# Half as many products of zeros in each unit of the first group, and another table of ranks, in a planned attention and expert kernel

## The chip, the cores and the metric

The kernel runs on one core of a Trainium2 chip. The metric is the device time of one execution in microseconds (us). Before the change it is 705.01 us, the median of three runs (704.97 to 705.55).

## The reference

Three layers follow each other. Causal attention over 2 batches, 8 heads, 576 tokens and 64 dimensions is mixed by a gate per head with a memory read; two dense layers with an ELU follow, and then four experts that are all computed and weighted by token.

```python
scores = np.where(causal, -1e9, (q @ k.T) / np.sqrt(D)); a = softmax(scores)
local = a @ v                                            # attention
mem_out = (phi(q) @ M_prev) / (phi(q) @ z_prev + 1e-6)   # phi(x) = elu(x) + 1
x = g * mem_out + (1 - g) * local                        # to 1152 x 512
h = x @ w_in;  x = elu(h) @ w_out                        # 512 -> 2048 -> 512
out = sum_e p[:, e] * (np.maximum(x @ w1[e], 0) @ w2[e]) # 4 experts, 512 -> 1024 -> 512
```

## The kernel before, in words

Every dense product is made of three (`mm3`, L319 to L321): numbers are split into a high and a low part, and high by high, low by high and high by low are summed in PSUM. The tiles are `ua` and `da` for the first dense pair, `ub` and `db` for the experts, with 384 or 512 columns. A weight block of 128x1024 is loaded, copied to its high part on ScalarE (`wh`, L283) and subtracted on GpSimd for the low part (`wl`, L287). The blocks of the first dense pair come as 64-bit numbers that are converted first: ScalarE's L263 and VectorE's L269 and L273. From block 5 on this conversion holds one of the two PSUM banks of the scores meanwhile (`cv`, tags `s0` and `s1`).

Attention is cut into units. Four units F0 to F3 (the first group) hold the first 192 tokens of both batches, one for each pair of heads; eight units R00 to R13 hold the rest, one for each batch and pair. A unit's steps are: load; split (`qh` on ScalarE, `ql` on GpSimd, on VectorE for F0); feature map `pp`; memory product into bank `om` (`mem`, L1331) with its division on VectorE; then for each of three query tiles a score (L1382), a masked minimum on VectorE (`lowest`, L1396) and an exponential on ScalarE (L1405); transposes in groups of four (`trans`, L1444) into the one PSUM bank `t`; its evacuation on ScalarE or VectorE in turn (`evac`, L1451 and L1449); value products into bank `ov` (L1460, L1467); the division, the sum with the memory part (L1499) and a last transposition (`turn`, L1505). F units also use banks of the three `m` for half of their scores and transposes; R units have `s0`, `s1` and `t` alone.

A planner (class `Plan`) fixes the order on each engine before anything runs. Every step has an engine, a cost, a rank and the steps that it follows; `MOVES` adds to ranks by family of step. Walking a modelled clock, it gives each engine the startable step of lowest rank. TensorE prefers to stay where it is, in attention or in dense work: it turns to the other kind only if the first startable step of its own kind ranks later by more than `STAY[0]` (in attention) or `STAY[1]` (in dense work). The engines then run these queues in order, and wait on semaphores.

TensorE also multiplies zeros: a product of zeros (`nothing`, L345) is 128x512 in bfloat16, writes a bank that the next step then overwrites, and stands there to keep TensorE busy. Eleven stand at the start (`warm`). `keep_busy(ps, least)` issues the larger of `least` and a number that the planner sets where its modelled TensorE waits over 0.3 us in the first 140 us. `FEWEST` is the `least` of a unit: one for F, none for R. A unit of F has it in six places: two of its three scores, the memory product, both groups of transposes, and the first value product.

Of the kernel before, what the change touches and what calls it, by code (L numbers as in the profile page):

```python
# [53 lines left out]


MOVES = {
# [15 lines left out]
}  # L72


# [19 lines left out]
def tile_kernel(  # L94
# [112 lines left out]
    FEWEST = {"F": 1, "R": 0}  # L207
# [136 lines left out]
    def nothing(ps):  # L344
        nc.tensor.matmul(  # L345
            ps.rearrange("p (n k) -> p n k", k=P), zeros, zeros.unsqueeze(1).to_broadcast([P, ps.shape[1] // P, P]),
            start=True, stop=True,
        )
# [3 lines left out]
    def keep_busy(ps, least=0):  # L352

        for _ in range(max(waits[0], least)):
            nothing(ps)
        waits[0] = 0

    def atile(shape, dtype, tag, name):
        return at["sbuf"].tile(shape, dtype, tag=tag, name=name, bufs=SLOTS[tag])

    def abank(tag, name):

        if tag == "m":
            return ps_m.tile([P, 512], F32, tag="m", name=name)
        return at[tag[0]].tile([P, 512], F32, tag=tag, name=name)
# [6 lines left out]
    class Moe1:  # L372

        parts, kind = NPART, "a"
# [169 lines left out]
    class Moe2(Moe1):  # L544

        parts, kind = 2 * E, "b"
# [234 lines left out]
    keep = {}  # L781
# [97 lines left out]
    class Wide1(Wide):  # L879
        parts, kind = NPART, "a"  # L880
# [117 lines left out]
    class Wide2(Wide):  # L998
        parts, kind = 2 * E, "b"
# [79 lines left out]
    def act_cost(n, psum=False):  # L1079
        return 0.833e-3 * n + (0.055 if psum else 0.095)  # L1080

    def dve_cost(n):
        return 1.042e-3 * n + 0.065
# [4 lines left out]
    def values_cost(kind, blocks):  # L1088

        return 0.06 * (kind == "F") + 0.203 * sum(2 if kind == "F" and (t, odd) == (2, 2) else 1 for t, odd, _ in blocks)  # L1090

    STAY = [18.6, 8.4]
    TURN = 0.09

    def attends(key):
# [2 lines left out]
    class Plan:  # L1098
# [4 lines left out]
        def __init__(self, slots):  # L1103
# [3 lines left out]

            self.stay = {True: STAY[0], False: STAY[1]}

# [100 lines left out]
    def segments(ext):  # L1210
        return [(0, ext)] if ext <= 512 else [(0, 288), (288, 576)]

    def plan_unit(plan, kind, b, c, start, spare, slack):
# [6 lines left out]
        unit, uid = {}, f"F{c}" if kind == "F" else f"R{b}{c}"  # L1220

        def parts_of(t):

            if kind == "F":
                return [(t, 0, P)] if t < 2 else [(0, 0, D), (1, D, D)]
            return [(0, 0, P)]

        def add(key, engine, cost, fn, after=(), takes=(), gives=()):
            step = key.rstrip("0123456789")
            plan.add(  # L1230
                (uid, key), engine, cost, start + OFFSET[step], fn,
                [(uid, a) if isinstance(a, str) else a for a in after], takes, gives,
                slack.get(engine, 0.0) + LANDING * (step in ("split_h", "phi_r") and uid not in ("F0", "F1")),
                early=EARLY if kind == "R" else 1e9,
            )
# [50 lines left out]
        for name, cs, loaded in splits:  # L1286
            n, first = cs.stop - cs.start, name == splits[0][0]
# [68 lines left out]
        def row(odd, t):  # L1356

            ext = tiles[t][1]
            first = 2 * base[t] + odd * ext
            return unit["pt"][:, first:first + ext]  # L1360

        def score(t, n):
            ext = tiles[t][1]
            a, z_ = segments(ext)[n]
            w = z_ - a
            if "pt" not in unit:
                unit["pt"] = atile([P, 2 * widest], F32, tag="pt", name=f"pt{uid}")[:, :2 * width]
                unit["nm"] = [atile([P, 6], F32, tag="nm", name=f"nm{uid}{odd}") for odd in (0, 1)]
            for odd in (0, 1):
                tag = "m" if "m" in s_from[t, n] else f"s{odd}"  # L1370
                unit["s", odd, t, n] = abank(tag, f"s{uid}{odd}{t}{n}")
            keep_busy(unit["s", 0, t, n], FEWEST[kind] * (t != 1))
            for bi, r0, r in parts_of(t):

                q = slice(qcol[t] + r0, qcol[t] + r0 + P)
                k0 = nq + bi * nkeys
                ks = slice(k0 + a, k0 + z_), slice(k0 + nkeys - ext + a, k0 + nkeys - ext + z_)
                final = r0 + r == P
                for m, (x, y) in enumerate(("hh", "hl", "lh")):
                    for odd in (0, 1):  # L1380
                        rows = slice(D * odd, D * odd + D)
                        nc.tensor.matmul(  # L1382
                            unit["s", odd, t, n][:, :w], unit[x][rows, q], unit[y][rows, ks[odd]],
                            start=m == 0 and r0 == 0, stop=m == 2 and final,
                        )
# [19 lines left out]
            nc.scalar.activation(out=blk, in_=blk, func=AF.Exp, scale=-1.0, bias=unit["nm"][odd][:, k:k + 1])  # L1405

        def score_cost(t, w):
            return len(parts_of(t)) * max(3 * w / 2400, 0.32) + 0.24 + 0.22 * FEWEST[kind] * (t != 1)

        for t, n, a, z_ in pieces:  # L1410
            first, last = (t, n) == pieces[0][:2], (t, n) == pieces[-1][:2]
# [23 lines left out]

        def transposes(g):
            pst = unit["t", g] = abank(t_from[g], f"t{uid}{g}")
            keep_busy(pst, FEWEST[kind])
            for n, (t, odd, j) in enumerate(groups[g]):
                if odd == 2:  # L1440
                    src = unit["pt"][:, 2 * base[t] + P * j:2 * base[t] + P * j + P]
                else:
                    src = row(odd, t)[:, P * j + D * odd:P * j + D * odd + P]
                nc.tensor.transpose(pst[:, P * n:P * n + P], src, ident)  # L1444

        def evac(g, col):
            pf = unit["p", g] = atile([P, 512], F32, tag="ph", name=f"pf{uid}{g}")
            if g % 2:
                nc.vector.tensor_copy(pf[:, :col], unit["t", g][:, :col])  # L1449
            else:  # L1450
                nc.scalar.activation(out=pf[:, :col], in_=unit["t", g][:, :col], func=AF.Copy)  # L1451
# [19 lines left out]
        for g, blks in enumerate(groups):  # L1471
            col, final = P * len(blks), g == len(groups) - 1
            add(
                f"trans{g}", "pe", 0.109 * len(blks) + 0.05 * (kind == "F") + 0.22 * FEWEST[kind], lambda g=g: transposes(g),
                sorted({f"exp{t}{odd}" for t, o, _ in blks for odd in ((0, 1) if o == 2 else (o,))})
                + [f"trans{g - 1}"] * (g > 0), [t_from[g]],
                ["pt"] * final,
            )
            add(
                f"evac{g}", "dve" if g % 2 else "act", dve_cost(col) if g % 2 else act_cost(col, True),  # L1480
                lambda g=g, col=col: evac(g, col), [f"trans{g}"], ["ph"],
                [("m", (uid, f"trans{g}")) if t_from[g] == "m" else "t"],
            )
            add(
                f"values{g}", "pe", values_cost(kind, blks) + 0.22 * FEWEST[kind] * (g == 0), lambda g=g: values(g),
                [f"evac{g}", "load_v"] + [f"values{g - 1}"] * (g > 0), ["ov"] * (g == 0), ["ph"] + ["rv", "nm", "nm"] * final,
            )
# [188 lines left out]
```

## Time and profile before

| | before |
|---|---|
| median of three runs | 705.01 us |
| the profiled execution | 705.03 us |
| its span, first to last instruction | 703.2 us |
| granted TensorE clock in every stretch | 1.00 (2.4 GHz) |
| TensorE busy | 697.8 us, 99% |
| VectorE, ScalarE, GpSimd busy | 387.7, 353.8, 426.6 us |

How to read it: the page's span leaves out 1.8 us of the execution. TensorE's busy time counts pipelined products from their start to a modelled end, so neighbours overlap; what a product costs the engine is the distance from its start to the next start, which the timeline shows. Matmuls in float32 (transposes, memory and value products) appear under their own lines.

### The profile page before, as it was taken

What the parts mean: (1) busy time and instruction counts of PE and PEld (TensorE: products, weight loads), DVE (VectorE), ACT (ScalarE), POOL (GpSimd) and SP (SyncE); (2) the same over time, 40 slices, a digit from 0 to 9 for tenths busy, and PEclk for the clock granted to TensorE, in tenths of its full rate; (3) what the DMA queues carried; (4) which work ended last, traced back from release to release, by engine and by line L of the source; (5) the groups of instructions that cost most, each with busy time, mean ns of one, the idle gap of its engine ahead of it and who ended that gap; (6) DMA issues with size and microseconds to landing.
All of it is one profiled execution on the core that took longest, in us unless ns stands there. A gap on an engine that the chain in (4) does not pass through costs nothing.

```text
span 703.2 us, 10662 instructions
## 1 busy us (share of the span) xinstructions
PE 697.8 (99%) x4064; PEld 638.8 (91%) x4064; DVE 387.7 (55%) x847; ACT 353.8 (50%) x611; POOL 426.6 (61%) x256
## 2 busy tenths in 40 slices
PE   9999999999999999999999999999999999999997
PEld 5788999999898998999999999999898989989896
DVE  5887878553434234723736648674554736455462
ACT  7889777654543335444865647633342424233220
POOL 6778766575554552599986564787655666464110
PEclk9999999999999999999999999999999999999999
DMA  8897877533413241234322212031121302111002
GB/s 279 293 307 248 291 243 255 185 121 127 139 60 122 90 131 49 91 119 136 121 64 87 90 45 75 32 116 65 60 91 31 119 29 93 61 60 61 1 0 90
DMA packets 23683, 82.21 MB, mean 117 GB/s; under 512 B 2896, under 2 KB 3152, under 8 KB 23632
## 3 DMA queue, kind: packets, MB, share of 16 engines
q1 hardware_dynamic: 23632, 81.53, 34.9%
q8 instruction: 32, 0.52, 0.3%
q14 instruction: 19, 0.16, 0.1%
HBM read 70.77 MB, written 10.75 MB: 116 GB/s over the span
## 4 chain that ended last, share of the span: by engine, by line
PE 96%; DVE 2%; ACT 1%; issue 0%; POOL 0%; POOLq 0%; DVEq 0%; ACTq 0%
PE db L319 9%; PE db L321 9%; PE db L320 9%; PE da L319 5%; PE da L321 5%; PE da L320 5%; PE ov L1460 4%; PE ub L319 3%; PE ub L321 3%; PE ub L320 3%; PE sR L1382 3%; PE tR L1444 3%; PE ua L319 2%; PE ua L321 1%; PE ua L320 1%; PE ov L1467 1%
## 5 line engine op out<-in xcount | busy, mean ns | idle before, releaser
L287 POOL TENSOR_TENSOR wl<-wr,wh 128x1024 fp32r<-128x1024 f32 x72 | 172.4, 2399 | 157.4 <-ACT wh L283 156.7
L283 ACT ACTIVATE wh<-wr 128x1024 fp32r<-128x1024 f32 x72 | 75.9, 1056 | 101.9 <-PE db L320 61.8
L319 PE MATMUL db<-wh,hb 128*128 128x512 f32 x288 | 112.7, 391 | 0.0
L321 PE MATMUL db<-wl,hb 128*128 128x512 f32 x288 | 112.4, 390 | 0.0
L320 PE MATMUL db<-wh,hb 128*128 128x512 f32 x288 | 112.3, 390 | 0.0
L1049 DVE SCALAR_TENSOR_TENSOR acc<-db,pr,acc 128x512 f32<-128x512 f32 x42 | 31.5, 750 | 70.8 <-PE db L321 70.8
L319 PE MATMUL da<-ha,wh 128*128 128x384 f32 x192 | 65.8, 343 | 0.0
L321 PEld LDWEIGHTS db<-wl,hb 128*128 128x128 f32 x288 | 54.1, 188 | 11.4
L321 PE MATMUL da<-ha,wh 128*128 128x384 f32 x192 | 64.3, 335 | 0.0
L320 PE MATMUL da<-ha,wl 128*128 128x384 f32 x192 | 64.2, 335 | 0.0
L319 PEld LDWEIGHTS db<-wh,hb 128*128 128x128 f32 x288 | 54.1, 188 | 10.8 <-issue 0.2
L320 PEld LDWEIGHTS db<-wh,hb 128*128 128x128 f32 x288 | 54.1, 188 | 10.7
L319 PE MATMUL ub<-yh,wh 128*128 128x384 f32 x128 | 44.6, 349 | 0.0
L321 PE MATMUL ub<-yl,wh 128*128 128x384 f32 x128 | 43.0, 336 | 0.0
L320 PE MATMUL ub<-yh,wl 128*128 128x384 f32 x128 | 42.8, 335 | 0.0
L1460 PE MATMUL ov<-rvR,pfR 128*128 128x65 f32 x288 | 38.6, 266 | 0.0
L1460 PEld LDWEIGHTS ov<-rvR,pfR 128*128 128x128 f32 x288 | 36.9, 191 | 0.9 <-issue 0.8
L557 ACT ACTIVATE hb<-ub 128x384 fp32r<-128x384 f32 x32 | 15.7, 490 | 43.8 <-PE ub L321 43.7
L319 PEld LDWEIGHTS da<-ha,wh 128*128 128x128 f32 x192 | 36.1, 188 | 0.7 <-issue 0.7
L320 PEld LDWEIGHTS da<-ha,wl 128*128 128x128 f32 x192 | 36.1, 188 | 0.0
L321 PEld LDWEIGHTS da<-ha,wh 128*128 128x128 f32 x192 | 36.0, 188 | 0.0
L560 DVE SCALAR_TENSOR_TENSOR hb<-ub,hb 128x384 fp32r<-128x384 f32 x32 | 17.8, 557 | 33.0 <-ACT hb L557 32.7
(859 smaller groups left out, 1833.5 us busy)
## 6 DMA issues: line engine op xcount, KB each, us to landing
wr<-in_w SPq DMA_DIRECT2D x64, 512.0 KB, 3.7
w<-in_w SPq DMA_DIRECT2D x32, 512.0 KB, 5.8
wscr<-wr SPq DMA_DIRECT2D x16, 512.0 KB, 6.5
wr<-wscr SPq DMA_DIRECT2D x16, 512.0 KB, 3.3
rvR<-in_vm_r SPq DMA_DIRECT2D x8, 520.0 KB, 4.6
qkR<-in_qk_r SPq DMA_DIRECT2D x8, 480.0 KB, 4.9
rvF<-in_vm_f SPq DMA_DIRECT2D x4, 520.0 KB, 6.1
out<-acc SPq DMA_DIRECT2D x8, 256.0 KB, 2.0
```

What stands on the lines that cost most here:

```text
L283: nc.scalar.activation(out=t["wh"], in_=t["wr"], func=AF.Copy)
L287: nc.gpsimd.tensor_tensor(out=wl, in0=t["wr"], in1=f32(t["wh"]), op=ALU.subtract)
L319: nc.tensor.matmul(out, ah, bh, start=first, stop=False)
L320: nc.tensor.matmul(out, al, bh, start=False, stop=False)
L321: nc.tensor.matmul(out, ah, bl, start=False, stop=last)
L557: nc.scalar.activation(out=t["h"][:, 0], in_=t["ps"], func=AF.Relu)
L560: nc.vector.scalar_tensor_tensor(out=t["h"][:, 1], in0=t["ps"], scalar=0.0, in1=f32(t["h"][:, 0]), op0=ALU.max, op1=ALU.subtract)
L1049: nc.vector.scalar_tensor_tensor(out=acc, in0=t["ps"], scalar=p, in1=acc, op0=ALU.mult, op1=ALU.add)
L1382: nc.tensor.matmul(unit["s", odd, t, n][:, :w], unit[x][rows, q], unit[y][rows, ks[odd]], start=m == 0 and r0 == 0, stop=m == 2 and final,)
L1444: nc.tensor.transpose(pst[:, P * n:P * n + P], src, ident)
L1460: nc.tensor.matmul(unit["ov"][:, odd, t], pf[:, col:col + P], unit["rv"][:, at_], start=False, stop=odd == 1 and j == nb - 1)
L1467: nc.tensor.matmul(pair("ov", t, r0, r), pf[:, col + r0:col + r0 + r], apart(at_), start=True, stop=nb == 0,)
```

## The change

`FEWEST` counts in three places of a unit instead of six: the memory product, the first group of transposes, and the first value product. The scores and the second group keep only what the planner asks for, and the planner's costs follow. `MOVES` has other entries and values throughout, and `STAY` is 86.268 and 0.703 instead of 18.6 and 8.4. Lines after the table are four higher in the changed kernel.

```diff
 MOVES = {
-    ("F", "evac"): -13.8, ("F", "join_l"): -16.9, ("F", "load"): -51.9, ("F", "mem_a"): 3.9, ("F", "phi_r"): 13,
...
+    ("F", "exp"): 1.027, ("F", "load"): -47.23, ("F", "lowest"): -22.121, ("F", "phi_r"): 12.499,
...
-    STAY = [18.6, 8.4]
+    STAY = [86.268, 0.703]
...
-            keep_busy(unit["s", 0, t, n], FEWEST[kind] * (t != 1))
+            keep_busy(unit["s", 0, t, n])
...
-            return len(parts_of(t)) * max(3 * w / 2400, 0.32) + 0.24 + 0.22 * FEWEST[kind] * (t != 1)
+            return len(parts_of(t)) * max(3 * w / 2400, 0.32) + 0.24
...
-            keep_busy(pst, FEWEST[kind])
+            keep_busy(pst, FEWEST[kind] * (g == 0))
```

The cost of `trans` in the planner gets the same factor `(g == 0)`.

Three places show what the new ranks do. The first is TensorE at unit R02's transposes, groups 1 to 3 (`tR021` to `tR023`), with its value products and the first score of R12. Before:

```order
L1444 MATMUL tR021_2090<-ident_66,ptR02_1898 128x128 x4
L1467 MATMUL ov_121<-rvR02_1591,pfR020_2078 128x130
L1460 MATMUL ov_121<-rvR02_1591,pfR020_2078 128x65 x3
L1382 MATMUL sR12000_2111<-qhR12_2041 128x288
L1382 MATMUL sR12100_2112<-qhR12_2041 128x288
L1382 MATMUL sR12000_2111<-qlR12_2074,qhR12_2041 128x288
L1382 MATMUL sR12100_2112<-qlR12_2074,qhR12_2041 128x288
L1382 MATMUL sR12000_2111<-qhR12_2041,qlR12_2074 128x288
L1382 MATMUL sR12100_2112<-qhR12_2041,qlR12_2074 128x288
L1444 MATMUL tR022_2122<-ident_66,ptR02_1898 128x128 x4
L1460 MATMUL ov_121<-rvR02_1591,pfR021_2103 128x65 x4
L319 MATMUL da0330_2135<-ha030_1654,wh15_1800 128x384
```

Eight more dense products follow this last row before `tR023`. After:

```order
L1448 MATMUL tR021_2031<-ident_66,ptR02_1857 128x128 x4
L1471 MATMUL ov_121<-rvR02_1572,pfR020_2020 128x130
L1464 MATMUL ov_121<-rvR02_1572,pfR020_2020 128x65 x3
L1448 MATMUL tR022_2050<-ident_66,ptR02_1857 128x128 x4
L1464 MATMUL ov_121<-rvR02_1572,pfR021_2043 128x65 x4
L1386 MATMUL sR12000_2069<-qhR12_2029 128x288
L1386 MATMUL sR12100_2070<-qhR12_2029 128x288
L1386 MATMUL sR12000_2069<-qlR12_2047,qhR12_2029 128x288
L1386 MATMUL sR12100_2070<-qlR12_2047,qhR12_2029 128x288
L1386 MATMUL sR12000_2069<-qhR12_2029,qlR12_2047 128x288
L1386 MATMUL sR12100_2070<-qhR12_2029,qlR12_2047 128x288
L1448 MATMUL tR023_2078<-ident_66,ptR02_1857 128x128 x4
```

The nine dense products between groups 2 and 3 are gone from there, and the score moved from ahead of group 2 to ahead of group 3. ScalarE at the same place, from the evacuation of group 0 (`pfR020`) to that of group 2 (`pfR022`). Before:

```order
L1451 ACTIVATE pfR020_2078<-tR020_2064 128x512
L283 ACTIVATE wh19_2087<-wr19_1910 128x1024
L503 ACTIVATE yh0_2100<-da0300_1987 128x384
L503 ACTIVATE yh0_2100<-da0310_2024 128x384
L503 ACTIVATE yh0_2100<-da0320_2049 128x384
L1451 ACTIVATE pfR022_2132<-tR022_2122 128x512
```

After, with the exponentials of R02 and the ELU of `ua` (L448 to L459) ahead and between:

```order
L287 ACTIVATE wh17_1995<-wr17_1909 128x1024
L459 ACTIVATE ha031_1937<-eva0u310_1979 128x384
L1409 ACTIVATE ptR02_1857<-ptR02_1857,nmR020_1858 128x320
L1409 ACTIVATE ptR02_1857<-ptR02_1857,nmR021_1859 128x320
L448 ACTIVATE eva0u320_2017<-ua0320_1984 128x384
L451 ACTIVATE eva0u320_2017<-eva0u320_2017 128x384
L1455 ACTIVATE pfR020_2020<-tR020_1973 128x512
L1254 ACTIVATE qhR12_2029<-qkR12_1485 128x960
L459 ACTIVATE ha032_1983<-eva0u320_2017 128x384
L448 ACTIVATE eva0u330_2045<-ua0330_2006 128x384
L451 ACTIVATE eva0u330_2045<-eva0u330_2045 128x384
L287 ACTIVATE wh18_2055<-wr18_1948 128x1024
```

`ha033` (L459) and `pfR022` (L1455) follow. The split of R12's keys, a weight block and ELU work now stand between the two evacuations. The second place is VectorE after F3's third score (`sF3020`, `sF3120`), whose minimum frees the banks `s0` and `s1` for R00. Before:

```order
L1396 ISA ptF3_498,nmF30_499<-sF3020_540,mask2_79 128x64
L1396 ISA nmF30_499 128x1
L1396 ISA ptF3_498,nmF31_500<-sF3120_541,mask2_79 128x64
L1396 ISA nmF31_500 128x1
L1306 SCALAR_TENSOR_TENSOR nv_F2_578<-ov_121,wloc_96 128x6
L1521 RECIPROCAL nv_F2_578<-nv_F2_578 128x6
L1312 TENSOR_TENSOR tvF2_582<-ov_121,nv_F2_578 128x2x3x64
L273 SCALAR_TENSOR_TENSOR wr1_385<-w64_1_0_293,wr1_385 128x512
L1396 ISA ptR00_584,nmR000_585<-sR00000_587,mask_71 128x288
```

After:

```order
L273 TENSOR_SCALAR wr1_437<-wr1_437 128x512
L277 SCALAR_TENSOR_TENSOR wr1_437<-w64_1_1_403,wr1_437 128x512
L1310 SCALAR_TENSOR_TENSOR nv_F2_568<-ov_121,wloc_96 128x6
L1525 RECIPROCAL nv_F2_568<-nv_F2_568 128x6
L1316 TENSOR_TENSOR tvF2_584<-ov_121,nv_F2_568 128x2x3x64
L1400 ISA ptF3_480,nmF30_481<-sF3020_536,mask2_79 128x64
L1400 ISA nmF30_481 128x1
L1400 ISA ptF3_480,nmF31_482<-sF3120_537,mask2_79 128x64
L1400 ISA nmF31_482 128x1
```

Two conversions of weight block 1 and F2's division moved ahead of the minimum. The third place is TensorE between F3's last value products and R00's memory product, which overwrites bank `om` once F3's last sum (L1499) has read it. Before:

```order
L1467 MATMUL ov_121<-rvF3_470,pfF31_614 64x130 x2
L319 MATMUL ua0000_653<-xh0_100,wh0_458 128x384
L320 MATMUL ua0000_653<-xh0_100,wl0_538 128x384
L321 MATMUL ua0000_653<-xl0_101,wh0_458 128x384
L319 MATMUL ua0000_653<-xh0_100,wh0_458 128x384
L320 MATMUL ua0000_653<-xh0_100,wl0_538 128x384
L321 MATMUL ua0000_653<-xl0_101,wh0_458 128x384
L1382 MATMUL sR00010_671<-qhR00_474 128x448
```

Five more score products and twelve more dense ones stand before the memory product there. After:

```order
L349 MATMUL sR00010_660<-zeros_93 128x512
L1386 MATMUL sR00010_660<-qhR00_477 128x448
L1386 MATMUL sR00110_661<-qhR00_477 128x448
L1386 MATMUL sR00010_660<-qlR00_521,qhR00_477 128x448
L1386 MATMUL sR00110_661<-qlR00_521,qhR00_477 128x448
L1386 MATMUL sR00010_660<-qhR00_477,qlR00_521 128x448
L1386 MATMUL sR00110_661<-qhR00_477,qlR00_521 128x448
L349 LDWEIGHTS zeros_93
L349 MATMUL om_120<-zeros_93 128x512
```

Another product of zeros stands ahead of this piece and another behind it, and then the memory product. All eighteen dense products that stood between moved behind it.

## Rows read from the trace of the kernel before

**Rows 1.** The page: busy time, share of the span and instructions of each engine

```profile
PE 697.8 (99%) x4064; PEld 638.8 (91%) x4064; DVE 387.7 (55%) x847; ACT 353.8 (50%) x611; POOL 426.6 (61%) x256
```

**Rows 2.** The waits of TensorE: who waited for whom, total us, times, longest

```profile
PE sF L345 <- DVE nmF L1396: 0.2, 1, 0.2
PE xF L1505 <- POOL tvF L1499: 0.2, 1, 0.2
```

**Rows 3.** Windows: length, busy us (count) by engine, clock, DMA share, GB/s

```profile
36.00:54.00 18.00, 17.94 (x132) 15.93 (x132) 15.77 (x39) 15.16 (x28) 13.11 (x8) 1.00 0.90 302
142.00:153.00 11.00, 11.00 (x76) 10.07 (x76) 7.02 (x21) 8.83 (x16) 8.09 (x6) 1.00 0.44 143
```

**Rows 4.** Timeline of TensorE: start, us to the last end, instructions

```profile
46.12 0.66 PE L1444 MATMUL tR<-ident,ptR 128*128 128x128 f32 x4
46.62 0.39 PE L1467 MATMUL ov<-rvR,pfR 128*128 128x130 f32 x2
...
48.04 0.60 PE L1444 MATMUL tR<-ident,ptR 128*128 128x128 f32 x4
48.48 1.00 PE L1460 MATMUL ov<-rvR,pfR 128*128 128x65 f32 x8
49.29 0.42 PE L319 MATMUL ua<-xh,wh 128*128 128x384 f32 x1
...
53.12 0.40 PE L1382 MATMUL sR<-qhR 64*128 64x288 f32 x2
...
53.72 0.45 PE L319 MATMUL ua<-xh,wh 128*128 128x384 f32 x1
54.00 0.34 PE L320 MATMUL ua<-xh,wl 128*128 128x384 f32 x1
54.18 0.34 PE L321 MATMUL ua<-xl,wh 128*128 128x384 f32 x1
...
54.88 0.27 PE L1444 MATMUL tR<-ident,ptR 128*128 128x128 f32 x1
...
55.21 0.78 PE L1460 MATMUL ov<-rvR,pfR 128*128 128x65 f32 x6
55.92 0.40 PE L1382 MATMUL sR<-qhR 64*128 64x288 f32 x2
```

**Rows 5.** Timeline of TensorE, two waits and a row of zeros

```profile
43.24 0.34 PE L321 MATMUL ua<-xl,wh 128*128 128x384 f32 x1
43.64 0.81 PE L345 MATMUL tR<-zeros 128*128 128x512 bf16 x3
44.29 0.60 PE L1444 MATMUL tR<-ident,ptR 128*128 128x128 f32 x4
...
116.02 0.72 PE L1382 MATMUL sR<-qhR 64*128 64x288 f32 x2
...
116.93 0.44 PE L319 MATMUL da<-ha,wh 128*128 128x384 f32 x1
```

**Rows 6.** Groups on ScalarE by form: busy us, mean ns of one, idle before

```profile
L283 ACT ACTIVATE wh<-wr 128x1024 fp32r<-128x1024 f32 x72 | 75.9, 1056 | 101.9 <-PE db L320 61.8 <-PE da L321 13.1 <-issue 7.1
L1451 ACT ACTIVATE pfR<-tR 128x512 f32<-128x512 f32 x24 | 14.2, 593 | 21.2 <-PE tR L1444 21.1
L455 ACT ACTIVATE ha<-eva0u 128x384 fp32r<-128x384 f32 x16 | 8.0, 515 | 2.7 <-DVE eva0u L450 2.7
```

**Rows 7.** Groups on VectorE by form

```profile
L269 DVE TENSOR_SCALAR cv<-cv 128x512 int32<-128x512 int32 x26 | 18.0, 694 | 4.8 <-ACT cv L263 4.8
L273 DVE SCALAR_TENSOR_TENSOR wr<-w,wr 128x512 int32<-128x512 int32 x6 | 5.1, 858 | 0.0
L1518 DVE COPY x<-xR 128x384 f32<-128x384 f32 x8 | 4.4, 555 | 5.9 <-PE xR L1505 5.3 <-ACT xB21h L1515 0.6
```

**Rows 8.** Timeline of VectorE, F3's division

```profile
37.78 0.15 DVE L1306 SCALAR_TENSOR_TENSOR nv_F<-ov,wloc 128x6 f32<-128x6 f32 x1
38.27 0.56 DVE L1312 TENSOR_TENSOR tvF<-ov,nv_F 128x384 f32<-128x384 f32 x1
```

More of the change, by code (lines that the diff above doesn't have):

```diff
@@ L1473, in plan_unit @@
             add(
-                f"trans{g}", "pe", 0.109 * len(blks) + 0.05 * (kind == "F") + 0.22 * FEWEST[kind], lambda g=g: transposes(g),
+                f"trans{g}", "pe", 0.109 * len(blks) + 0.05 * (kind == "F") + 0.22 * FEWEST[kind] * (g == 0), lambda g=g: transposes(g),
                 sorted({f"exp{t}{odd}" for t, o, _ in blks for odd in ((0, 1) if o == 2 else (o,))})
```

32 rows, old and new, of the table MOVES are left out of this document.

## The prediction

> **What bounds the kernel now.** I read the page first: TensorE is busy for 99% of the span, no other engine for more than 61% [rows 1]. Busy time of pipelined products can hide gaps, so the waits come next: beside the start of the program TensorE's list holds two waits of 0.2 us each [rows 2]. The timeline gives what the list misses, by distances from start to start. A dense product of 384 columns costs 0.175 us (four from 54.18 to 54.88) [rows 4]. The one at 43.24 takes 0.40 to the next start, so 0.22 is a wait; the scores at 116.02 take 0.91 to the next start where others take 0.60 (53.12 to 53.72), so 0.31 is a wait [rows 4, 5]. So the kernel is bound by the row of products on TensorE, and about 0.9 us of waits is all that a new order can take out. What it can add has no such limit. The windows show why the middle is the place to look: from 142 to 153 us ScalarE is busy 8.83 of 11 us, and TensorE never stands, since dense products lie between the steps that need ScalarE [rows 3].
>
> **The change, part by part.** The sum is made against the profiled execution, 705.03 us (span 703.2 and 1.8 around it), which agrees with the median of 705.01.
>
> *The zeros.* The order of before holds 40: 11 warm ones, 24 that `FEWEST` asks for, and 5 that the planner adds where it models a wait. Taking out 12 of 24 would save 2.6 us at 0.217 each (three from 43.64 to 44.29) [rows 5]. But the new order holds 40 as well: 11, 12, and 17 from the planner. Two of these have 384 columns, so the gain is 0.1 us. Ahead of the first dense product there were 37 and are 35; five stand at unit R11, near 117 us. Where a zero falls into a real wait it is free. It is not where it must wait for the same bank as the step behind it.
>
> *Turns of TensorE.* Counted in the two orders: runs of dense products entered from attention work fall from 67 to 57. A run of six takes 1.16 us, 53.72 to 54.88, against 1.05 for six at 0.175 [rows 4]: 0.11 each, so -1.1. Scores entered from other work go from 41 to 42. Value products ahead of scores take 0.71 for six records (55.21 to 55.92) where eight ahead of dense work take 0.81 (48.48 to 49.29), 0.10 more for a switch [rows 4]: +0.1. Float32 work straight behind scores goes from 17 to 23; four transposes take 0.50 there (46.12 to 46.62) and 0.44 behind dense work (48.04 to 48.48) [rows 4]: +0.36. With the zeros I take -0.74. The ends are -1.2, without the two additions, and -0.1, if a run saved is worth half, because the float32 product that ends early at a turn gives part back.
>
> *Waits that go.* The new order has other work at all three places, so 0.2 at L1505, 0.22 and 0.31 fall away: -0.73 [rows 2, 4, 5]. The ends are -0.73 and -0.4, since a like wait can come elsewhere. The wait of 0.2 at F0's third score has the same steps ahead of it and stays.
>
> *New waits.* Four places have too little TensorE work in front of a step that another engine releases. The trace of before has none of the four waits, so each is bounded by what is queued on both sides.
>
> (a) R02's transposes, the first place shown. There is one bank `t`, so group 3 waits until ScalarE has evacuated group 2. Behind the end of group 2 ScalarE still has a weight block (1.06), `ha033` (0.52) and the evacuation (0.59), 2.17 together [rows 6]. TensorE has eight records of value products (0.81) and one score (0.60), 1.41 [rows 4]. The wait is 0.76 if ScalarE begins then; overlap of neighbours takes some, and I use 0.65. Group 1 has 24 dense products in front (4.2), against a weight block, `ha031`, two exponentials and two ELU steps (about 0.52 each, taken from `ha`) and the evacuation, 4.3 [rows 6]: 0.1 to 0.5, I use 0.35. Together 1.0. The ends are 0, if ScalarE runs ahead, and 1.7, if it is one block behind. What is queued on TensorE behind the wait is R12's scores, which then start ScalarE's and VectorE's next work later.
>
> (b) R00's first score waits for bank `s0`, which VectorE frees with F3's last minimum, the second place shown. Ahead of that minimum it now has two conversions (about 0.69 and 0.86) [rows 7] and a division (1.05, 37.78 to 38.83) [rows 8], 2.6 together. TensorE has eight records of value products (0.81), three zeros (0.65) and four transposes (0.44), 1.9. I use 0.5; the ends are 0 and 0.9.
>
> (c) R00's memory product waits for bank `om`, the third place shown. F3's division and sum take 1.05 and about 0.56 behind the last value product [rows 8]. TensorE has two zeros (0.43) and one score (0.6, wider here) instead of 18 dense products. I use 0.5; the ends are 0.3 and 0.7.
>
> (d) The third score of R11 waits for a bank that weight block 13 holds during its conversion. VectorE has a copy of R01's result (0.56) and two conversions (0.69 each) behind that unit's turn [rows 7], 1.9. TensorE has six records of the memory product (0.6) and three dense products (0.6). I use 0.7; the ends are 0.2 and 1.2. The three zeros there write the same bank, so they follow the wait and don't fill it.
>
> The new waits are 1.0 + 0.5 + 0.5 + 0.7 = 2.7, with ends 0.5 and 4.5. The sum is 705.03 - 0.74 - 0.73 + 2.7 = 706.26, say 706.3 us: 1.3 us or 0.18% longer. About 0.2% (1.4 us) is what a measurement of this kernel can tell from no change, so this forecast lies just inside it.
>
> **The rivals.**
>
> *The other engines run ahead.* If ScalarE and VectorE reach the four places early, the new waits are at their lower ends and the fewer turns win: 705.03 - 1.2 - 0.73 + 0.5 = 703.6. For it: no engine but TensorE is over 61% busy [rows 1]. Against it: ScalarE's share at 142 to 153 us is 80% [rows 3], and the queued work at each place is what the price is made of, not the average.
>
> *One bank for transposes becomes the bound of the attention runs.* With `STAY[0]` at 86 the planner keeps TensorE in attention. Pairs of consecutive groups of an R unit with no dense product between them rise from 7 to 12 in the orders. If each of the five added pairs waits as group 3 in (a) does, 0.65 each, that is 3.3 in place of (a)'s 1.0, and the time is 708.6. Half of it gives 707.4, and the sign "slower" is decided from about 1.2 us for (a) on. For it: the evacuations alternate between ScalarE and VectorE, and one weight block of 1.06 in the queue suffices [rows 6]. Against it: some of the pairs have a score or a memory product between them, 0.6 each, and the next evacuation is then often on VectorE, which is busy 7.02 of 11 us [rows 3].
>
> *The clock falls.* The granted clock is 1.00, the level of 2.4 GHz, also around the stretch from 44.29 to 53.72, which holds attention work with three dense products at a time and no zeros; there dense products stay at 0.175 [rows 3 to 5]. If the first 30 us lost the clock for 5 us, products started in it would take twice the distance, and some 2.5 us would be added: 708.8. The number of zeros ahead of the first dense product hardly differs, 37 and 35, so I give this little. The Trainium skill (TensorE: Matmul & The Clock Gate, section Part 4: PE-mode transpose) says that transposes don't count as busy for the clock gate in the way that other products do, which speaks against taking zeros away from in front of transposes. The trace agrees only in part: it has transposes 0.11 apart at the full level, with dense work near. By that rule the time would be this rival's.
>
> *The change doesn't do what it says.* In zeros it indeed does not, 40 against 40; that is in the forecast, and the new order is all that counts.
>
> **How the numbers follow.** The forecast's own case, (a) to (d) near the values used, has 0.48 within 0.2%; it reaches from 704.8 to 706.4. The other engines running ahead: 0.10, below 703.6. The single bank, (a) above 1.2 or (b) and (d) at their upper ends: 0.38. The clock: 0.04. So faster 0.10, same 0.48, slower 0.42. All terms at their ends would give 703.6 and 709.0 (705.03 - 0.1 - 0.4 + 4.5); ends of like sign at once are unlikely. I take 704.3 to 708.2, which leaves half of the first rival and the top of the second outside.
>
> **What the changed kernel's profile would show.** Right: waits of TensorE near 31 us (L1386), 37 us (L349 of `om`), 117 us (L349 of `sR`) and 147 to 151 us (L1448), released by VectorE three times and then by ScalarE's L1455, 2.7 us in all; the three waits of before gone; the rest of the row of products a little shorter. Wrong: no wait over 0.2 us at R02's transposes; waits over 1 us anywhere; a granted clock under 1.00, or dense products 0.35 apart, in the first 40 us; or new waits behind 155 us, where the forecast has none.

## The result, and the profile after

The changed kernel takes 715.45 us (median of 5 runs, 715.04 to 716.33) against 705.01 for the kernel before in the same session: a ratio of 1.0146, 95% interval 1.0132 to 1.016. It is 10.4 us slower, and the forecast of 706.3 us with its range up to 708.2 was wrong. In the page, TensorE's row answers to [rows 1], the clock's row to the table of before; lines of the changed kernel's code stand 4 higher than before.

```profile
span 713.5 us, 10666 instructions
PE 702.4 (98%) x4064; PEld 642.2 (90%) x4064; DVE 391.6 (55%) x847; ACT 353.6 (50%) x611; POOL 424.7 (60%) x256
PEclk9899999999999999999999999999999999999999
```

The span grew by 10.3 us (703.2 before). TensorE's busy time grew by 4.6 (697.8 to 702.4) and its idle time by 5.7 (5.4 to 11.1), although it runs the same count of products. The list of TensorE's waits, which answers to [rows 2], names most of the idle time (columns: us in total, times, longest):

```profile
PE tF L349 <- DVE xl L1517: 2.2, 1, 2.2
PE ub L323 <- DVE hb L564: 2.2, 1, 2.2
PE warm L349 <- DVE zeros L145: 1.0, 1, 1.0
PE sR L349 <- DVE wr L277: 0.7, 1, 0.7
PE tR L1448 <- ACT pfR L1455: 0.6, 2, 0.3
PE om L349 <- DVE tvF L1503: 0.4, 1, 0.4
PE sF L349 <- DVE nmF L1400: 0.2, 1, 0.2
```

Of the lower rows, `sR`, `tR` and `om` are forecast waits; `warm` and the last stand in both kernels. The fourth forecast wait, of R00's first score, isn't in the list. The two upper rows were not forecast. Windows over these two places, each the wait and what follows it (columns as in [rows 3]):

```profile
27.10:29.33 2.23, 0.04 (x3) 0.06 (x2) 2.20 (x5) 1.62 (x2) 1.36 (x1) 1.00 0.99 384
29.33:36.60 7.27, 7.27 (x38) 5.03 (x37) 4.66 (x21) 4.89 (x10) 1.48 (x2) 0.53 0.54 181
289.87:292.04 2.17, 0.00 (x1) 0.00 (x1) 2.14 (x5) 1.43 (x4) 0.29 (x1) 1.00 0.51 134
292.04:295.60 3.56, 3.56 (x12) 3.56 (x13) 1.09 (x2) 1.68 (x3) 2.60 (x2) 0.55 0.25 100
```

In each pair TensorE first stands for 2.2 us while VectorE is busy all the time (third busy column), and then the granted clock is close to 0.5, the level of 1.2 GHz. Products of 384 columns then start 0.32 us apart instead of 0.175 [rows 4], as two at the second place show:

```profile
293.22 0.52 PE L324 MATMUL ub<-yh,wl 128*128 128x384 f32 x1
293.54 0.52 PE L325 MATMUL ub<-yl,wh 128*128 128x384 f32 x1
```

In the trace the lower level lasts 6.8 us at the first place and 3.4 at the second. That is the growth of the busy time: half of 10.2 is 5.1, the most that it can cost, and 4.6 was found. So 4.4 us of waits and 4.6 us of the lower clock make 9.0 of the 10.3.

Why is VectorE late at the first place? Its timeline there, then GpSimd's (start, us, instruction):

```profile
23.52 1.23 DVE L273 TENSOR_SCALAR wr<-wr 128x512 int32<-128x512 int32 x1
24.78 2.65 DVE L277 SCALAR_TENSOR_TENSOR wr<-w,wr 128x512 int32<-128x512 int32 x1
27.36 0.72 DVE L273 TENSOR_SCALAR wr<-wr 128x512 int32<-128x512 int32 x1
28.11 0.69 DVE L277 SCALAR_TENSOR_TENSOR wr<-w,wr 128x512 int32<-128x512 int32 x1
28.72 0.55 DVE L1517 TENSOR_TENSOR xl<-xF,xh 128x384 fp32r<-128x384 f32 x1
```

```profile
23.46 1.00 POOL L1503 TENSOR_TENSOR tvF<-tvF,tmF 128x384 f32<-128x384 f32 x1
24.66 2.23 POOL L1260 TENSOR_TENSOR qlR<-qkR,qhR 128x960 fp32r<-128x960 f32 x1 [0.20 <-ACT qhR L1254]
26.86 1.61 POOL L1275 TENSOR_SCALAR ppR<-qkR 128x384 f32<-128x384 f32 x1
```

The merge at 24.78 takes 2.65 us where its twin at 28.11 takes 0.69. It began 0.12 us after GpSimd's subtraction for R00 and ended 0.54 after it: it stood until GpSimd was done, and a standing instruction is counted as busy. TensorE waits for the last row, which frees the bank. The second place shows the same with the sums of T3, here VectorE, then GpSimd:

```profile
285.39 5.19 DVE L773 TENSOR_TENSOR xT<-x 128x384 f32<-128x384 f32 x2
291.44 1.13 DVE L564 SCALAR_TENSOR_TENSOR hb<-ub,hb 128x384 fp32r<-128x384 f32 x2
```

```profile
285.10 5.06 POOL L291 TENSOR_TENSOR wl<-wr,wh 128x1024 fp32r<-128x1024 f32 x2 [0.71 <-ACT wh L287]
```

Two sums, each 0.55 us in its shortest case, take 5.19 beside two subtractions of weight blocks. A list by form gives the comparison within one line of code (minimum, median and maximum in ns):

```profile
L277 DVE SCALAR_TENSOR_TENSOR wr<-w,cv x26: 675/687/689, 50.8 to 133.9; 128x512 int32<-128x512 int32 x26
L277 DVE SCALAR_TENSOR_TENSOR wr<-w,wr x6: 689/692/2653, 20.8 to 51.4; 128x512 int32<-128x512 int32 x6
```

The form with one input in PSUM (`cv`, a bank) never stretches in 26 cases; the form with both in SBUF does. The Trainium skill (SBUF — State Buffer, section Who interferes with whom) says that a VectorE instruction with two SBUF inputs contends with a GpSimd instruction that reads SBUF, and that what they share is an exclusive lock. These two rows agree with it.

### The profile page after: what moved, and what is told of

Same layout as the page of the kernel before. It is cut to its first block, busy times and chain, and to the rows that moved or that the text cites. A ratio compares the mean times of both kernels' runs of the same rounds, so it can differ in the third digit from the quotient of the medians.

```text
span 713.5 us, 10666 instructions
## 1 busy us (share of the span) xinstructions
PE 702.4 (98%) x4064; PEld 642.2 (90%) x4064; DVE 391.6 (55%) x847; ACT 353.6 (50%) x611; POOL 424.7 (60%) x256
## 4 chain that ended last, share of the span: by engine, by line
PE 80%; DVE 2%; ACT 1%; issue 0%; DVEq 0%; ACTq 0%
PE db L323 9%; PE db L325 9%; PE db L324 9%; PE da L323 4%; PE da L324 4%; PE da L325 4%; PE ub L323 3%; PE ub L324 3%; PE ub L325 3%; PE ov L1464 2%; PE tR L1448 2%; PE sR L1386 1%; DVE xT L773 1%; PE ov L1471 1%; PE pb17S L324 0%; PE pb16S L323 0%
## 5 line engine op out<-in xcount | busy, mean ns | idle before, releaser
L325 PEld LDWEIGHTS db<-wl,hb 128*128 128x128 f32 x288 | 54.0, 188 | 11.4
L1409 ACT ACTIVATE ptR<-ptR,nmR 128x576 f32<-128x576 f32 (+2 forms) x48 | 29.9, 661 | 12.8 <-DVE nmR L1400 12.6
```

What stands on the lines that cost most here:

```text
L325: nc.tensor.matmul(out, ah, bl, start=False, stop=last)
```

## The experiments

Three theories stood at the start: (1) VectorE stands behind GpSimd at the two places, TensorE waits, and the idle stretch lets the clock fall; (2) fewer zeros let the clock fall by themselves; (3) VectorE is late because of a weight block's load. All runs are compared with the kernel before on the same chip: e3, e5, e7 and e8 ran on one, where it took 704.89 us, the others on another, where it took 705.11 to 705.13.

**e1: GpSimd's subtraction for R00 in four pieces.**

```
-            eng.tensor_tensor(out=unit["l"][:, cs], ...)
+            n = 4 if uid == "R00" else 1
+            step = (cs.stop - cs.start) // n
+            for c0 in range(cs.start, cs.stop, step):
+                ps = slice(c0, c0 + step)
+                eng.tensor_tensor(out=unit["l"][:, ps], ...)
```

> The changed kernel, with the subtraction of qlR for unit R00 on GpSimd (128x960, 2.23 us in one piece at 24.66 us) cut into four pieces of 240 columns; nothing else differs. Theory 1 (VectorE stands while a GpSimd instruction runs, TensorE waits 2.19 us for it at 29.33 us, and that idle stretch lets the clock fall): the VectorE shift-and-merge at 24.78 us, 2.65 us long, shortens to 1.0 or less, the wait at tF falls from 2.2 to 0.8 or less, the clock stays at 1.00 from 29.3 to 36.6 us; 715.4 - 1.5 - 3.4 = 710.5 us (709.5 to 711.7). Theory 2 (fewer products of zeros let the clock fall, whatever the wait): the wait may go, the clock still shows 0.5 for 6.8 us; 713.9 us. Theory 3 (VectorE is late because a weight block's load is late): the VectorE instruction and the wait stay; 715.4 us.

711.6 us (710.46 to 712.69). VectorE, GpSimd, and TensorE's wait in this kernel:

```profile
24.78 1.12 DVE L277 SCALAR_TENSOR_TENSOR wr<-w,wr 128x512 int32<-128x512 int32 x1
27.76 0.54 DVE L1521 TENSOR_TENSOR xl<-xF,xh 128x384 fp32r<-128x384 f32 x1
```

```profile
24.65 3.74 POOL L1264 TENSOR_TENSOR qlR<-qkR,qhR 128x240 fp32r<-128x240 f32 x4 [0.18 <-ACT qhR L1254]
```

```profile
PE ub L323 <- DVE hb L564: 2.2, 1, 2.2
PE tF L349 <- DVE xl L1521: 1.2, 1, 1.2
```

Nothing but the size of GpSimd's pieces changed, and the merge fell from 2.65 to 1.12 us. That is theory 1; a late load (theory 3) would have left it. The wait shrank to 1.2, more than the 0.8 expected: the next conversion of either kind stretched beside the later pieces, to 0.92 and 1.06 us. The clock stayed at 1.00 behind the first place and still fell behind the second:

```profile
28.35:36.00 7.65, 7.50 (x63) 5.82 (x62) 6.61 (x28) 6.86 (x14) 4.85 (x5) 1.00 0.91 292
288.40:292.00 3.60, 3.60 (x13) 3.60 (x14) 1.06 (x2) 1.65 (x3) 2.67 (x2) 0.57 0.18 72
```

**e2: the subtractions of weight blocks 39 and 40 in four pieces each.**

```
-            nc.gpsimd.tensor_tensor(out=wl, in0=t["wr"], ...)
+            step = 256 if i in (39, 40) else 1024
+            for c0 in range(0, 1024, step): ...
```

> The changed kernel, with the subtraction of wl for weight blocks 39 and 40 on GpSimd (128x1024, 2.40 and 2.70 us in one piece, from 285.1 us) cut into four pieces of 256 columns each. Theory 1: the two sums of T3 on VectorE, 5.19 us together at 285.39 us, shorten to 3 us or less, TensorE's wait of 2.17 us for hb at 292.0 us goes, the clock stays at 1.00 there; 715.4 - 2.2 - 1.7 = 711.5 us (710.5 to 712.5). Theory 2 says nothing on this place, where no products of zeros were removed, and theory 3 expects no change: 715.4 us (714.7 to 716).

712.01 us (709.95 to 712.44). VectorE at the second place:

```profile
285.68 1.87 DVE L776 TENSOR_TENSOR xT<-x 128x384 f32<-128x384 f32 x2
287.47 2.11 DVE L776 TENSOR_TENSOR xT<-x,xT 128x384 f32<-128x384 f32 x2
```

The first two sums fell from 5.19 to 1.87 us (the next two took 2.11 where they had taken 1.01), TensorE's wait for `hb` and the fall of the clock behind it are gone, and the first place is as it was.

**e4: the changed kernel's order and table, with zeros at six places again.**

```
-            keep_busy(unit["s", 0, t, n])
+            keep_busy(unit["s", 0, t, n], FEWEST[kind] * (t != 1))
...
-            keep_busy(pst, FEWEST[kind] * (g == 0))
+            keep_busy(pst, FEWEST[kind])
```

> The changed kernel's order and its table, with the products of zeros issued at all six places of a unit of the first group again (nine products more than in the changed kernel). Theory 1: the waits at 29.3 and 292.0 us are made by VectorE and GpSimd and stay, and the clock still falls after both; 715.4 plus 0 to 1.5 us for the added products: 716 us (715 to 717). Theory 2: the clock stays at 1.00 from 29.3 to 36.6 us; 715.4 - 3.4 + 0.7 = 712.7 us (712 to 713.5).

711.82 us (711.53 to 712.15), below both, nearer to theory 2. The clock stayed at 1.00 throughout, but it also stayed behind the second place, 250 us from the nearest added zero, with the same wait as before. Windows of that wait and what follows:

```profile
288.05:290.20 2.15, 0.00 (x1) 0.00 (x0) 2.12 (x5) 1.41 (x4) 0.29 (x1) 1.00 0.50 171
290.20:294.00 3.80, 3.79 (x19) 3.52 (x20) 1.67 (x3) 3.02 (x5) 2.81 (x2) 1.00 0.18 71
```

So an idle stretch of 2.2 us can let the clock fall and need not. The first wait was 1.5 us here, as TensorE came to it later, so this run doesn't tell at the first place whether the zeros or the shorter wait held the clock. The table by itself, with all zeros in place, costs 711.82 - 705.13 = 6.7 us.

**e6: ten zeros into a bank that nobody reads, ahead of each of the two waits.**

```
+            if (uid, g) == ("F2", 1):
+                spare_bank = abank("t", "fillA")
+                for _ in range(10):
+                    nothing(spare_bank)
             keep_busy(pst, FEWEST[kind] * (g == 0))
```

> The changed kernel with ten products of zeros into a bank that nobody reads ahead of each of the two waits (before the second group of transposes of F2, and before the first-layer products of part 5, unit 3, of the second layer pair). Theory 1 (it is the idle stretch that lets the clock fall): the products fill the two waits of 2.2 us, TensorE has no idle of over 0.5 us there, VectorE is as late as before, and the clock stays at 1.00 after both; 715.4 - 3.4 - 1.7 = 710.3 us (709.5 to 711.3). Theory 2 (only the number of zeros early in the kernel counts): the first fall goes, the second stays: 712.0 us. If the clock falls for a reason that TensorE's own work does not set: 715.4 us.

711.22 us (710.89 to 711.63). TensorE at the first place, and windows, of what follows the first fill and of the second fill with what follows it:

```profile
27.00 2.33 PE L349 MATMUL fillA<-zeros 128*128 128x512 bf16 x10
29.26 0.59 PE L349 MATMUL tF<-zeros 128*128 128x512 bf16 x2
```

```profile
29.50:36.60 7.10, 6.95 (x60) 5.38 (x58) 6.09 (x25) 6.85 (x14) 3.37 (x3) 1.00 0.77 233
287.00:292.50 5.50, 5.50 (x28) 3.89 (x27) 3.58 (x7) 3.94 (x8) 2.65 (x2) 1.00 0.38 125
```

VectorE is as late as before, TensorE's next step starts as late, but TensorE is busy in between, and the clock stays at 1.00 at both places. The gain of 4.2 us against the changed kernel is near the 4.6 by which the lower clock lengthened TensorE's busy time; 5.1 was expected.

**e3: both cuts.** The edits of e1 and e2 together.

> The changed kernel with both cuts: GpSimd's subtraction for R00 in four pieces and its subtractions for weight blocks 39 and 40 in four pieces each. Theory 1 (each place costs by itself what its cut gave back: 715.5 - 711.6 = 3.9 us and 715.5 - 712.0 = 3.4 us): 715.5 - 3.9 - 3.4 = 708.2 us (707.3 to 709.2), clock 1.00 throughout, waits of 1.2 us and none. If one cut only moves the loss to the other place: 711 to 712 us.

708.22 us (707.77 to 709.65), as worked out: the two places add up. The second wait is gone, the clock stays at 1.00, and the longest wait is

```profile
PE tF L352 <- DVE xl L1524: 1.2, 1, 1.2
```

**e7: the second wait later**, by eight zeros at one dense group of the second layer pair.

```
-                        keep_busy(t["ps"])
+                        keep_busy(t["ps"], 8 * ((self.name, part, fc, nb) == ("b0", 2, 0, 0)))
```

> The changed kernel with eight products of zeros more in the dense products, about 70 us ahead of the second long wait, so that this wait of 2.2 us comes some 1.7 us later in the program and is otherwise the same; the place at 29 us is untouched. It asks why the clock stayed at 1.00 after the second wait in the kernel with six zeros. Theory 1a (an idle stretch of 2.2 us always lets the clock fall): both falls as in the changed kernel, 715.5 + 8 x 0.21 = 717.2 us (716.4 to 718). Theory 1b (whether it falls after the same stretch hangs on when the stretch comes): the fall at 29 us stays, the one at 292 us can go: 717.2 - 1.5 = 715.7 us. Theory 2 says that nothing but the zeros of the first 60 us matters: 717.2 us.

714.52 us (712.91 to 715.87). Windows of the second wait and what follows it:

```profile
291.99:294.15 2.16, 0.00 (x1) 0.00 (x0) 2.13 (x5) 1.41 (x4) 0.30 (x1) 1.00 0.55 180
294.15:298.00 3.85, 3.83 (x20) 3.53 (x21) 1.67 (x3) 3.07 (x5) 2.86 (x2) 1.00 0.18 72
```

The wait comes 2.1 us later than in the changed kernel (1.7 was expected) and is as long, and the clock stayed at 1.00: theory 1b. The zeros of the first 60 us were the changed kernel's, and the fall at 29 us is there. What decides it is left open. The trace is of the execution of 715.87 us; two of the four took 712.91 and 713.24, below all that was expected, and have no trace.

**e10: VectorE's subtraction for F1's bank ahead of the first half of weight block 1.** The two instructions of that half (`lower` like `shift`) are kept back until `join` has been issued:

```
         def shift(half):
+            if (i, half) == (1, 0):
+                later.append(lambda: shift_now(half))
...
+                while uid == "F1" and later:
+                    later.pop(0)()
```

> The changed kernel with that swap on VectorE alone: GpSimd's subtractions stay in one piece. It asks whether the loss at the first place lies in the instruction of GpSimd or in what stood behind it. Theory 1: VectorE's shift-and-merge still stands for 2.6 us beside GpSimd's subtraction, but only 0.8 us or less of TensorE's wait of 2.2 us is left and the clock stays there; 715.5 - 1.4 - 2.7 = 711.4 us (710.5 to 712.5). If TensorE waits for the data of the stretched instruction itself: 715.5 us.

710.85 us (710.33 to 715.99).

```profile
24.49 2.65 DVE L290 SCALAR_TENSOR_TENSOR wr<-w,wr 128x512 int32<-128x512 int32 x1
27.06 0.54 DVE L1530 TENSOR_TENSOR xl<-xF,xh 128x384 fp32r<-128x384 f32 x1
```

```profile
PE ub L336 <- DVE hb L577: 2.2, 1, 2.2
PE tF L362 <- DVE xl L1530: 0.8, 1, 0.8
```

The merge stands for the same 2.65 us, but the step that TensorE waits for comes earlier, and the wait is 0.8 (a new one of 0.4 stands at the next scores). It is the queue behind a standing instruction that costs. Four of the six executions had a mean clock of 0.999 or 1.000 and took 710.3 to 711.1 us; one had 0.992 and took 715.99. So one and the same kernel moves by 5 us from one execution to another, and its clock with it; the waits of that one are not on record.

**e9: both cuts and that swap.**

> The changed kernel with both cuts (R00's subtraction and those of weight blocks 39 and 40) and with VectorE's subtraction for F1's bank, which the first wait of TensorE hangs on, placed ahead of the first half of weight block 1 instead of behind it (two instructions, 0.9 and 1.1 us); no other instruction moves. Theory 1: the wait of 1.2 us that was left goes too, and what is left of the change is the sum that was forecast for it without the two places: 708.2 - 1.2 = 707.0 us (706.2 to 707.8; the forecast was 706.3). If the wait only moves to the next bank: 708.2 us.

707.65 us (707.57 to 708.62). The wait for the bank is gone, and one of 0.8 us stands at the next scores instead:

```profile
PE 698.0 (99%) x4064; PEld 639.0 (91%) x4064; DVE 388.7 (55%) x847; ACT 353.4 (50%) x611; POOL 427.5 (61%) x265
```

```profile
PE sF L1406 <- DVE nmF L1420: 0.8, 1, 0.8
...
PE sR L1406 <- DVE nmF L1420: 0.2, 1, 0.2
```

TensorE's busy time is 698.0 us, that of before 697.8 [rows 1].

**e5, e8 and e11: the kernel before with fewer zeros**, in its own order: three places (10 fewer), none of the six (22 fewer, not the 24 expected, since the planner itself asks for two of them), all six in unit F0 only (18 fewer). The edit is the second argument of `keep_busy`, which in e8 `keep_busy` ignores; no other instruction differs.

> The kernel before, with its order and its table, and the products of zeros issued at three places of a unit of the first group where there were six: ten fewer, and no other instruction on any engine differs. Theory 1 (the order that the new table makes is what cost; the zeros by themselves only take TensorE's time): 705.1 - 10 x 0.21 = 703.0 us (702.4 to 704.4), clock 1.00 throughout, no TensorE wait over 1 us. Theory 2 (fewer zeros let the clock fall): a stretch at 0.5 in the first 60 us, 708 us or more. If the zeros stood in TensorE's waits: 705.1 us.

> The kernel before, with its order and its table, without the 24 products of zeros that stand at the six places of the first group's units whether or not a wait was foreseen; the 11 at the start and the 5 that were put in for foreseen waits stay. Theory 1: the clock stays at 1.00 as long as TensorE has no long wait; 705.1 - 24 x 0.21 = 700.1 us if all of them stood on TensorE's path, up to 704 us where waits come out in their place (700 to 704). Theory 2 (the number of zeros holds the clock): a fall in the first 60 us, 706 us or more.

> The kernel before, with its order and its table; the products of zeros at the six places stay in the first of the first group's four units, F0, alone (18 fewer). It asks which of the zeros stood in TensorE's waits and which only took its time, and whether the falls of the clock within the first 25 us, which the two kernels with fewer zeros showed, come from the first unit. Theory 1: the clock stays at 1.00, the zeros of F1 to F3 gave back at most what all 24 gave (0.8 us); 704.2 us (703.6 to 705). Theory 2 (the number of zeros holds the clock, wherever they stand): a fall within the first 60 us and 705 to 707 us.

e5: 704.84 us (ratio 1.0007, 0.9998 to 1.0016). e8: 704.11 us (0.9992, 0.9983 to 1.0001). e11: 704.37 us (0.9998, 0.9987 to 1.0009). None can be told from the kernel before, so no version here beats it; the 703.0 and 700.1 that theory 1 allowed for e5 and e8 did not come. All three show falls of the clock in part of their executions (a mean clock of 0.998 or less in 7 of 11, 9 of 11 and 4 of 11; in none of the 38 of the kernel before beside them). Two windows and a row of e5:

```profile
16.00:17.00 1.00, 1.00 (x6) 0.84 (x5) 1.00 (x6) 0.88 (x3) 0.97 (x1) 0.50 0.93 369
17.00:20.40 3.40, 3.40 (x25) 2.63 (x24) 2.27 (x6) 3.27 (x8) 1.14 (x1) 0.77 1.01 374
```

```profile
14.31 0.30 PE L1382 MATMUL sF<-qhF 64*128 64x64 f32 x2 [0.34 <-DVE nmF L1396]
```

Behind the start of the program and ahead of that fall no wait is longer than 0.34 us, so theory 2 has its place: in the first units the zeros do hold the clock, by their number or because short waits like this one open where they stood, which these runs don't tell apart. It isn't by itself what made the changed kernel slow, whose clock is at 1.00 from 5.7 to 29.5 us. And 22 zeros fewer gave back 0.8 us, not 4.6: in e8's trace TensorE's busy time fell by 3.8 us and its idle time grew by 2.8, so most of them stood in waits.

The two parts of the change don't add up: ten zeros fewer cost nothing that can be measured in the order of before (e5), the table costs 6.7 us with all zeros (e4), and the two together cost 10.4. The other 3.6 came where nine zeros fewer met the new order: the first wait was 2.2 us instead of 1.5, and the clock fell behind both long waits.

## Why the prediction was wrong, point by point

*What bounds the kernel.* Right: TensorE's row of products, and a new order can only add waits without limit.

*The zeros, 40 and 40.* Right. With the same 40 the clock stays at 1.00 once the long waits are cut (e3, e9), so their number is not the cause by itself.

*Turns of TensorE, -0.74, and waits that go, -0.73.* The first is wrong in sign. Busy time can't show it (698.0 in e9, 697.8 before), since a product ahead of a wait counts as busy to its modelled end. Distances from start to start, summed over these two traces from the first score on and without the waits in them, can: dense products take 1.2 us less in e9, much as the ten runs fewer were priced (1.1), but attention's products and the zeros take 1.9 more, where +0.36 was priced. So the row got some 0.7 us longer. What a run of dense products saved, attention's side of the turn took back: in both traces a group's last value product takes 0.08 us ahead of a dense product and 0.205 ahead of a score. The prediction knew of this only for its upper end (which by its own terms is -0.19, not -0.1). The three waits went, and one of 0.2 came at 11.4 us.

*New waits, 2.7 with ends 0.5 and 4.5.* The four places were right. By the list, which counts idle time alone: (d) 0.7 as forecast, (c) 0.4 for 0.5, (a) 0.6 for 1.0, and (b) 0.2 for 0.5, the second row of e9's waits; in the changed kernel itself it doesn't show. Together 1.9; by distances in e9, 2.4. e9 without its remaining wait of 0.8 is 706.85 us, against 706.3. That this is so near is in part luck: the 1.4 us by which the turns were off is half hidden by a start of the program that was 0.8 us shorter (e9's first score is at 5.84 us, that of before at 6.62).

*The step that failed* is the sentence "Four places have too little TensorE work in front of a step that another engine releases". It looked for places by counting queued work at mean durations, [rows 6, 7], as if a duration belonged to an instruction. Two more places had enough work in front by that count, and lost 2.2 us each since a VectorE instruction stood behind GpSimd. At the first, the four conversions ahead of F1's subtraction are 2.8 us at the means of before (0.56 and 0.86, twice) and took 5.2; at the second, two sums are 2.3 us at the mean of 1.15 and took 5.19. Either excess is more than the whole wait. The sum had no term for these 4.4 us, and none for the 4.6 us of lower clock that came behind them: 9.0 of the 10.3 together. The mean of 858 ns in [rows 7] was the warning. By form, the trace of before has:

```profile
L273 DVE SCALAR_TENSOR_TENSOR wr<-w,wr x6: 680/785/1201, 16.5 to 45.0; 128x512 int32<-128x512 int32 x6
L769 DVE TENSOR_TENSOR xT<-x x4: 546/628/2784, 289.3 to 296.3; 128x384 f32<-128x384 f32 x4
```

A sum of 546 ns that once takes 2784 was there to see. Before, TensorE did not wait for it (ScalarE did); the new order put TensorE's next step behind it.

*The rival "the clock falls", 708.8 at 0.04.* The price per place was of the right kind (2.5 for 5 us at the lower level), the condition was wrong: it was tied to the number of zeros ahead of the first dense product, and here it was tied to the two waits (e6 fills them and keeps the clock). It got 0.04 because that number hardly differs, and the sum held no long wait that could have spoken for it. No run puts the rule on transposes that was weighed there to a test.

*The other rivals.* Engines running ahead: (a) at 0.6 lies between. The single bank: (a) is 0.6, so no.

*What would show it wrong* named no wait over 0.2 us at R02's transposes, waits over 1 us, dense products 0.35 apart or a clock under 1.00 in the first 40 us, and waits behind 155 us. The first did not come (0.25 and 0.34). The others did: two waits of 2.2 us, the clock at 0.5 from 29.6 us on, and one of the waits at 290 us. Dense products stood 0.32 apart only at 293 us. The range had made no room for them.

## What to carry to other kernels

Read minimum and maximum beside the mean of each form: an instruction whose longest case is several times its shortest may be standing behind another engine, as here behind GpSimd, and a new order can put the critical step behind it. Where VectorE and GpSimd both work on SBUF, look at what is queued behind the pair; a cut of GpSimd's instruction, or the released step placed first, took most of the loss away here. Price a wait of TensorE of a few us with its clock: in the changed kernel 4.4 us of waits brought 4.6 more, in e4 waits of 2.2 and 1.5 us brought nothing.

## What the runs showed of the hardware

- VectorE beside GpSimd: a merge of 0.69 us took 2.65 beside a subtraction of 2.23; two sums of 0.55 took 5.19 beside 5.06 of GpSimd. The stand counts as busy time. It isn't only instructions with two inputs in SBUF: in e4 a shift with one, 0.42 us in its shortest case, took 2.46 (from 26.01 us on) beside that subtraction.
- The cut has a price on GpSimd: 960 columns take 2.23 us in one piece and 3.74 in four, the stands behind VectorE between them included.
- After equal idle stretches of 2.2 us the clock fell to the level of 1.2 GHz in the profiled runs of the changed kernel, e1 and e2 and stayed at that of 2.4 GHz in e4, e7 (at the second place) and e10; in e10 it differed from one execution to the next. In e5 it fell with no wait over 0.34 us ahead of it.
